# Sliding-window attention and gated MLP: values times probabilities once per pair of heads, in two PSUM banks shared with the transposes

## The chip, the cores and the metric

The kernel runs on one core of a Trainium2 chip, with its engines TensorE (PE; PEld is its loading of weights), VectorE (DVE), ScalarE (ACT), GpSimd (POOL) and the DMA queues that SyncE (SP) issues. The metric is the time of one execution on the device in microseconds; smaller is better.

## The reference

Attention with 4 batches, 8 heads, 768 positions and 64 elements a head. A query sees the 4 first keys (sinks) and the 128 keys that end with its own. The result, laid out as 512 columns a position, goes through an MLP with 1024 inner columns and a gate that comes from a convolution over three positions.

```python
scores = scale * np.matmul(q, k.transpose(0, 1, 3, 2))
is_sink = pos[None, :] < int(n_sink)          # n_sink = 4
rel = pos[:, None] - pos[None, :]
in_window = (rel >= 0) & (rel < int(window))  # window = 128
scores = np.where(is_sink | in_window, scores, -1000000000.0)
a = softmax(scores)
x = (a @ v) as (B, S, H * D)
h = np.maximum(x @ w_in, 0.0)
conv_out += conv_w[k] * hp[:, k:k + S, :]     # k = 0, 1, 2
out = (h * sigmoid(conv_out)) @ w_out
```

All is float32. Where the kernel wants float32 accuracy from one pass of PE, it splits an operand into a high and a low part (names ending in H and L) and adds three products; other float32 products take two passes.

## The kernel before, in words

`banded` works on pairs of heads, `g` = 0 to 15: 4 batches of 4 pairs (`NPAIR` = 4). A pair has 6 tiles of 128 queries, `t` = 0 to 5, in two halves of three tiles (`hf`, `u`). Batch 0 runs all first halves of its four pairs and then all second halves; later batches (`g >= NPAIR`) run a pair's two halves one behind the other. The main loop has one step `i` for each tile and three slots in a step: `scores` of tile i, `transp` of the tile before, `pv` of the tile before that (delays `D1` = 1, `D2` = 2).

- `scores(g, t)` makes scores of a tile for both heads (sc, L334 to L338), masks them on DVE (L502, L503), takes exponents on ACT (L506) and normalises on POOL (L511) into `pe`.
- `transp(g, t)` turns the two 128 x 128 blocks of probabilities with PE into a slot of `pts` in PSUM (L526), and one ACT copy (L528) brings them to the key tile's `pT` in SBUF. `pT` of key tile kt holds, for both heads, the block of query tile kt and that of query tile kt + 1, since the window reaches one tile back; POOL's two selects (L530, L532) cut the two triangles from the one block. At a half's last tile the sinks' probabilities are turned as well (`sT`, L540 or L548).
- `pv(g, t)` does nothing except at a half's last tile. There it multiplies values by the probabilities of the half's key tiles into `px`, one PSUM bank with 3 x 128 columns (L567): the values of one head are 64 columns of weights, so that the two heads lie in partitions 0 to 63 and 64 to 127. The sinks' products are added (L570). Key tile 2 is needed by both halves (query tiles 2 and 3), and has a `pT` for each.
- `xout` then copies px to the high part of x on ACT (xH, L345), and DVE subtracts for the low part (xL, L346).

In between, the loop places pieces of the MLP of the batch before (`fill`, from `Moe.pieces`): products with w_in (ph, L183), the gate on ACT, DVE and POOL (L190 to L201), products with w_out (po, L210). A batch's pieces are made when the `pv` of its last pair has been written down, and are spread over the next 24 steps; those of the last batch come at the end with no attention beside them. This written order is not yet the order of the engines: the program is built with a scheduler that lays out each engine's instructions by its own simulated times, and puts waits where tiles, buffers and PSUM banks require them.

PSUM has eight banks: two for sc, one for pts, one for px, two with tag h, two for po. `PTB` is the number of pT buffers.

Of the kernel before, what the change touches and what calls it, by code (L numbers as in the profile page):

```python
# [10 lines left out]
F32 = mybir.dt.float32  # L11
F32R = mybir.dt.float32r
# [5 lines left out]
P = 128  # L18
D = 64
NEG = 1.0e9  # L20
NS = 4
SP = 16
SR = 6 * NS
KW = P + NS
SW = 2 * P + NS
CH = 256
NT = CH // P
PTB = 6
RAWB = 4
PLAIN = 4  # L30
ORDER = [("k", 0), ("k", 1), ("q", 0), ("q", 1)]
# [6 lines left out]
def f(ap):  # L38
    return ap.bitcast(F32)
# [353 lines left out]
def banded(c):  # L393

    nc = c.nc
    m = Moe(c)
    A = Attn(c, m.x, KW, m.mp, m.ps)
    T = A.T
    NPAIR = c.H // 2
    NG = c.B * NPAIR  # L400
    cp = c.es.enter_context(c.tc.tile_pool(name="bc", bufs=1))
    ap, ps = A.ap, A.ps
# [30 lines left out]
    vsr = cp.tile([3 * SR, 3, NPAIR * P], F32R, name="vsr")  # L433
# [18 lines left out]
    A.settle = lambda: m.need(len(m.raws))  # L452
    st = [Ctx() for g in range(NG)]
    for s in st:
        s.pe, s.pT, s.raw, s.X = {}, {}, {}, [None, None]
    st[0].v = c.v_raw[0]

    jobs = [(g, half) for half in range(2) for g in range(NPAIR)]
# [18 lines left out]
            st[g].raw[nm, half] = load_half(c, g, nm, half, c.raw[asked[0] % RAWB])  # L477
            asked[0] += 1

    pts = ps.tile([P, 2, 2, P], F32, name="pts")  # L480

    def scores(g, t):
        s = st[g]
# [29 lines left out]
    def keytile(g, kt, hf):  # L513

        s = st[g]
        if (kt, hf) not in s.pT:
            s.pT[kt, hf] = ap.tile([P, 2, 2, P], F32, tag="pT", name=f"pT{g}_{kt}_{hf}", bufs=PTB)
        return s.pT[kt, hf]

    def transp(g, t):  # L520
        s = st[g]
        hf, u = divmod(t, 3)
        pt = pts[:, A.n % 2]
        A.n += 1
        for j in range(2):
            nc.tensor.transpose(pt[:, j, :], s.pe[hf][:, u, j, NS:KW], c.ident)  # L526
        own = keytile(g, t, hf)[:, :, 0]
        nc.scalar.copy(own, pt)  # L528
        if t:
            nc.gpsimd.affine_select(out=keytile(g, t - 1, hf)[:, :, 1], in_=own, pattern=[[0, 2], [-1, P]],  # L530
                                    compare_op=ALU.is_gt, fill=c.zero, base=0, channel_multiplier=1)
            nc.gpsimd.affine_select(out=own, in_=own, pattern=[[0, 2], [1, P]], compare_op=ALU.is_ge, fill=c.zero,  # L532
                                    base=0, channel_multiplier=-1)
        if u == 2:
            pk = m.ps.tile([P, P], F32 if g < NPAIR else F32R, tag="h", name=f"tk{g}_{t}", bufs=2)
            sinks = s.pe[hf].rearrange("p t h k -> p (t h) k")
            if g < NPAIR:
                sk = ap.tile([P, 6, SP], F32, tag="sk", name=f"sk{g}_{hf}")
                nc.scalar.copy(sk, sinks[:, :, 0:SP])
                nc.tensor.transpose(pk[0:6 * SP, :], sk.rearrange("p t k -> p (t k)"), c.ident)  # L540
                s.sT = ap.tile([6 * SP, P], F32, tag="sT", name=f"sT{g}_{hf}")
                nc.scalar.copy(s.sT, pk[0:6 * SP, :])  # L542
                return
            sk = ap.tile([P, 3, 6, NS], F32R, tag="sk", name=f"sk{g}_{hf}")
            sinks = sinks[:, :, 0:NS]
            nc.scalar.copy(sk[:, 0:3:2], sinks.rearrange("p (o t) k -> p o t k", o=1).to_broadcast([P, 2, 6, NS]))
            nc.vector.tensor_tensor(out=sk[:, 1], in0=sinks, in1=f(sk[:, 0]), op=ALU.subtract)
            nc.tensor.transpose(pk[0:3 * SR, :], sk.rearrange("p a t k -> p (a t k)"), c.identr)  # L548
            s.sT = ap.tile([3 * SR, P], F32R, tag="sT", name=f"sT{g}_{hf}")
            nc.scalar.copy(s.sT, f(pk[0:3 * SR, :]))  # L550

    def pv(g, t):

        s = st[g]
        hp = g % NPAIR
        hf, u = divmod(t, 3)
        if u < 2:
            return
        px = ps.tile([P, 3, P], F32, tag="px", name=f"px{g}_{hf}").rearrange("p t k -> p (t k)")
        first = 3 * hf  # L560
        tiles = range(first + 2, max(0, first - 1) - 1, -1)
        for kt in tiles:
            pT = s.pT.pop((kt, hf)).rearrange("p h a k -> p h (a k)")
            lo, hi = max(kt, first), min(kt + 1, first + 2)
            cols = slice(P * (lo - kt), P * (hi - kt) + P)
            for j in range(2):
                nc.tensor.matmul(px[D * j:D * j + D, P * (lo - first):P * (hi - first) + P], s.v[:, kt, j, :], pT[:, j, cols],  # L567
                                 start=(kt == tiles[0]), stop=False, skip_group_check=True)
        for w in range(1 - hf, 3):
            nc.tensor.matmul(px[:, P * w:P * w + P], (vsr if g >= NPAIR else c.vs)[:, w, P * hp:P * hp + P], s.sT, start=False, stop=(w == 2),  # L570
                             skip_group_check=True)
        A.xout(g, hf, px)

    kks = []

# [44 lines left out]
    cuts = {NSTB // 2: (0, 1, NSTB // 2), NSTB: (1, m.NCH, NSTB)}  # L620
# [3 lines left out]
    for i in range(NST + D2):  # L624
        if i < NST:
            n, g, t = steps[i]
# [15 lines left out]
        for slot in range(SLOTS):  # L642
            if slot == 0 and i < NST:
                scores(g, t)
            if slot == 1 and 0 <= i - D1 < NST:
                transp(*steps[i - D1][1:])
            if slot == 2 and 0 <= i - D2 < NST:
                pv(*steps[i - D2][1:])
                if i - D2 + 1 in cuts:
                    while fill:  # L650
                        fill.pop(0)()
                    lo, hi, span = cuts[i - D2 + 1]
                    fill = m.pieces(lo, hi)
                    rate = len(fill) / (span - 0.5)
                    acc = 0.0
            acc += rate / SLOTS
            while acc >= 1.0 and fill:
                fill.pop(0)()
                acc -= 1.0
            while todo and i + (slot + 1) / SLOTS >= todo[0][0]:  # L660
                todo.pop(0)[1]()
# [73 lines left out]
def attention_gated_mlp(ctx: ExitStack, tc: tile.TileContext, q, k, v, n_sink, window, w_in, conv_w, w_out, out):  # L735
# [33 lines left out]
    with tc.If(fast == 1) as cmp:  # L769
        with ExitStack() as es:  # L770
            c.es = es
            banded(c)
# [32 lines left out]
```

## Time and profile before

| what | value |
|---|---|
| median of 3 runs | 490.8 us (489.17 to 491.21) |
| profiled execution, its time | 491.53 us |
| profiled execution, its span | 489.8 us |
| mean granted TensorE clock | 0.991 |
| instructions | 10503 |
| busy share of PE, DVE, ACT, POOL | 93%, 70%, 70%, 64% |
| HBM read, written | 27.60 MB, 6.29 MB |

The span is from the first to the last instruction. A group's row gives the line, engine, operation, output and inputs, shapes and count, then busy us and the mean ns of one, then the idle time of the engine ahead of it and what ended it. Matmuls overlap, and their ends are modelled: what one costs is read from the distance of starts. In the timeline, neighbours of one kind are merged (x16), and a row in brackets tells the idle time before.

### The profile page before, as it was taken

Reading aid. Unit: us, or ns where it says so; the run is one execution under the profiler, and the core shown is the slowest. Engines: PE = TensorE matmul, PEld = TensorE weight load, DVE = VectorE, ACT = ScalarE, POOL = GpSimd, SP = SyncE. Lnnn points to the kernel's source line nnn. Section 1 sums busy time; section 2 is a strip of 40 time slices with the busy share of each in tenths; the row PEclk is TensorE's granted clock in tenths of the full one; section 3 lists DMA queues with packets and bytes.
Section 4 is the critical chain, followed back from the end, with each engine's and each line's share of the span. In section 5 each row is a group of like instructions: output and inputs, shape, how many; then the busy total and the mean of one; then the engine's idle time right before and its main releaser. Section 6 shows DMA issues by size and latency. Waiting matters only on the chain.

```text
span 489.8 us, 10503 instructions
## 1 busy us (share of the span) xinstructions
PE 457.6 (93%) x3149; PEld 388.8 (79%) x3149; DVE 343.8 (70%) x1211; ACT 344.3 (70%) x1087; POOL 314.0 (64%) x614
## 2 busy tenths in 40 slices
PE   1877698999999999999999999999999999999993
PEld 1644577778888888998888887898888888999982
DVE  4689989857768777776677778686776574655561
ACT  3888877869867978887768877785867664545541
POOL 3396688856876868695657667585765564444341
PEclk9999979999999999999999999999999999999999
DMA  5687744547234141433231421333120100101001
GB/s 145 188 250 205 187 146 84 135 91 184 52 81 115 62 115 33 101 96 83 73 86 35 107 68 34 71 92 85 45 58 8 45 2 1 44 1 43 26 20 51
DMA packets 87307, 41.01 MB, mean 84 GB/s; under 512 B 80161, under 2 KB 80185, under 8 KB 87241
## 3 DMA queue, kind: packets, MB, share of 16 engines
q1 hardware_dynamic: 87240, 40.25, 32.0%
q8 instruction: 27, 0.44, 0.4%
q14 instruction: 40, 0.32, 0.2%
HBM read 27.60 MB, written 6.29 MB: 69 GB/s over the span
## 4 chain that ended last, share of the span: by engine, by line
PE 83%; POOL 4%; DVE 3%; ACT 3%; DMA 3%; issue 2%; SPq 1%; DVEq 0%; ACTq 0%; POOLq 0%
PE ph L183 28%; PE po L210 27%; PE px L567 8%; PE pts L526 4%; PE sc L337 4%; PE sc L338 3%; PE px L570 2%; PE tq L271 2%; POOL pe L511 2%; PE sc L334 2%; PE tk L289 1%; DMA raw<-in_k_dram 1%; POOL wiL L122 1%; DMA sc_i<-in_window_dram 1%; POOL pT L530 1%
## 5 line engine op out<-in xcount | busy, mean ns | idle before, releaser
L210 PE MATMUL po<-woH,g 128*128 128x512 f32 x384 | 142.2, 410 | 1.2 <-POOL g L200 1.2
L183 PE MATMUL ph<-xH,wiH 128*128 128x258 f32 (+1 forms) x384 | 112.7, 293 | 1.2 <-ACT sT L542 1.2
L183 PE MATMUL ph<-xH,wiL 128*128 128x258 f32 (+1 forms) x384 | 110.0, 287 | 0.0
L183 PE MATMUL ph<-xL,wiH 128*128 128x258 f32 (+1 forms) x384 | 109.4, 285 | 0.0
L511 POOL TENSOR_SCALAR pe<-pe,sm 128x132 f32<-128x132 f32 (+1 forms) x192 | 86.0, 459 | 30.4 <-DVE sm L509 19.1
L200 POOL TENSOR_SCALAR g<-t 128x256 fp32r<-128x256 f32 x96 | 41.9, 437 | 79.1 <-DVE t L198 59.0
L506 ACT ACTIVATE pe<-pe,sm 128x132 f32<-128x132 f32 (+1 forms) x192 | 77.5, 407 | 16.6 <-DVE sm L503 15.2
L195 DVE SCALAR_TENSOR_TENSOR t<-hb,cw,t 128x256 f32<-128x256 f32 x96 | 55.5, 579 | 35.5 <-ACT t L194 34.4
L210 PEld LDWEIGHTS po<-woH,g 128*128 128x128 f32 x384 | 69.0, 189 | 12.1 <-POOL g L200 2.6
L183 PEld LDWEIGHTS ph<-xH,wiH 128*128 128x128 f32 x384 | 73.2, 191 | 6.6 <-ACT sT L542 2.0
L201 POOL TENSOR_TENSOR g<-t,g 128x256 fp32r<-128x256 f32 x96 | 74.3, 774 | 5.4
L210 PE MATMUL po<-woL,g 128*128 128x512 f32 x192 | 76.6, 399 | 0.0
L183 PEld LDWEIGHTS ph<-xH,wiL 128*128 128x128 f32 x384 | 73.3, 191 | 2.2
L183 PEld LDWEIGHTS ph<-xL,wiH 128*128 128x128 f32 x384 | 73.3, 191 | 0.9
L197 ACT ACTIVATE t<-t 128x256 f32<-128x256 f32 x96 | 40.3, 420 | 34.7 <-DVE t L196 34.4
L502 DVE COPY_PREDICATED sc<-before,sc 128x128 f32<-128x128 int32 x160 | 44.9, 291 | 25.7 <-PE sc L338 20.5
L198 DVE SCALAR_TENSOR_TENSOR t<-t,hb 128x256 f32<-128x256 f32 x96 | 47.0, 490 | 21.1 <-ACT t L197 20.2
L503 DVE CUSTOM_DVE_ANT_0 pe<-sc,m 128x132 f32<-128x132 f32 (+1 forms) x192 | 52.6, 288 | 10.1 <-PE sc L338 7.8
L196 DVE SCALAR_TENSOR_TENSOR t<-hb,cw,t 128x256 f32<-128x256 f32 x96 | 55.6, 579 | 4.4
L530 POOL TENSOR_SCALAR_AFFINE_SELECT pT<-pT 128x256 f32<-128x256 f32 x80 | 39.2, 490 | 29.5 <-ACT pT L528 25.2
L190 ACT ACTIVATE hb<-ph 128x258 f32<-128x258 f32 (+1 forms) x96 | 37.0, 385 | 29.3 <-PE ph L183 27.8
L194 ACT ACTIVATE t<-hb,cw 128x256 f32<-128x256 f32 x96 | 49.2, 513 | 7.1 <-POOL g L201 3.3
(123 smaller groups left out, 918.4 us busy)
## 6 DMA issues: line engine op xcount, KB each, us to landing
raw<-in_q_dram SPq DMA_DIRECT2D x64, 96.0 KB
raw<-in_k_dram SPq DMA_DIRECT2D x64, 96.0 KB
out_dram<-stm SPq DMA_DIRECT2D x24, 256.0 KB
kk<-kk SPq DMA_DIRECT2D x24, 198.0 KB
vraw<-in_v_dram SPq DMA_DIRECT2D x24, 192.0 KB
wi_0r<-in_moe_w_in_dram SPq DMA_DIRECT2D x2, 512.0 KB
wi_1r<-in_moe_w_in_dram SPq DMA_DIRECT2D x2, 512.0 KB
wi_2r<-in_moe_w_in_dram SPq DMA_DIRECT2D x2, 512.0 KB
```

The source lines that it names most:

```text
L183: nc.tensor.matmul(u.h[:, 0:W], w[:, cc, ff * P:(ff + 1) * P], x[:, cc, t0:t1], start=(i == 0), stop=(i == len(prods) - 1))
L194: nc.scalar.mul(a, prev, cw[:, 0, ff:ff + 1])
L195: nc.vector.scalar_tensor_tensor(out=e, in0=this, scalar=cw[:, 1, ff:ff + 1], in1=a, op0=ALU.mult, op1=ALU.add)
L196: nc.vector.scalar_tensor_tensor(out=a, in0=nxt, scalar=cw[:, 2, ff:ff + 1], in1=e, op0=ALU.mult, op1=ALU.add)
L198: nc.vector.scalar_tensor_tensor(out=a, in0=e, scalar=1.0, in1=this, op0=ALU.add, op1=ALU.mult)
L201: nc.gpsimd.tensor_tensor(out=u.g[:, 1], in0=a, in1=f(u.g[:, 0]), op=ALU.subtract)
L210: nc.tensor.matmul(po[:, 0:c.DM], u.g[:, a, tt * P:(tt + 1) * P], w[:, ff, :], start=(ff == 0 and i == 0), stop=(ff == NFF - 1 and i == 2))
L502: nc.vector.copy_predicated(pc[:, KW:SW], before.bitcast(I32), pc[:, 0:P])
L503: nc.vector.tensor_tensor_reduce(out=pe[:, j, cols], in0=pc[:, P:SW][:, cols], in1=mk, op0=ALU.add, op1=ALU.min, scale=1.0, scalar=3.0e38, ...
L506: nc.scalar.activation(pe[:, j, cols], pe[:, j, cols], AF.Exp, bias=sm[:, j:j + 1], scale=-1.0, accum_out=sm[:, 2 + 2 * j:3 + 2 * j])
L511: nc.gpsimd.tensor_scalar(pe[:, j, cols], pe[:, j, cols], sm[:, 8 + j:9 + j], 1.0, ALU.mult, ALU.mult)
L530: nc.gpsimd.affine_select(out=keytile(g, t - 1, hf)[:, :, 1], in_=own, pattern=[[0, 2], [-1, P]], compare_op=ALU.is_gt, fill=c.zero, base= ...
```

## The change

For later batches `pv` acts only at the pair's last tile (t = 5) and makes all six tiles of x at once, into `pb`, a PSUM tile of two banks (1024 columns): x takes columns 0 to 767. The last 256 columns, in the second bank, are `pts`, which held two slots before and holds one now. `px` is gone. Key tile 2 of a later pair has one pT in place of two, so a pair has six, all held until `pv`; `PTB` goes from 6 to 7. A product that would reach over the edge of the two banks is cut in two there (`cuts`). The sinks' probabilities of the first half are kept (`sT` for each half). The two halves of x are then copied out one behind the other. In batch 0 the halves stay as they were, with x in the first bank.

```diff
-PTB = 6
+PTB = 7
...
-    pts = ps.tile([P, 2, 2, P], F32, name="pts")
+    pb = ps.tile([P, 2 * T // 3, 2, P], F32, name="pb").rearrange("p t h k -> p (t h k)")
+    pts = pb[:, T * P:T * P + 2 * P].rearrange("p (h k) -> p h k", h=2)
...
     def keytile(g, kt, hf):
         s = st[g]
+        hf = hf if g < NPAIR else 0
...
     def transp(g, t):
-        pt = pts[:, A.n % 2]
-        A.n += 1
         for j in range(2):
-            nc.tensor.transpose(pt[:, j, :], s.pe[hf][:, u, j, NS:KW], c.ident)
+            nc.tensor.transpose(pts[:, j, :], s.pe[hf][:, u, j, NS:KW], c.ident)
         own = keytile(g, t, hf)[:, :, 0]
-        nc.scalar.copy(own, pt)
+        nc.scalar.copy(own, pts)
...
     def pv(g, t):
-        if u < 2:
+        if u < 2 or (g >= NPAIR and hf == 0):
             return
-        px = ps.tile([P, 3, P], F32, tag="px", name=f"px{g}_{hf}").rearrange("p t k -> p (t k)")
-        first = 3 * hf
-        tiles = range(first + 2, max(0, first - 1) - 1, -1)
-        for kt in tiles:
-            pT = s.pT.pop((kt, hf)).rearrange("p h a k -> p h (a k)")
-            lo, hi = max(kt, first), min(kt + 1, first + 2)
-            cols = slice(P * (lo - kt), P * (hi - kt) + P)
-            for j in range(2):
-                nc.tensor.matmul(px[D * j:D * j + D, P * (lo - first):P * (hi - first) + P], s.v[:, kt, j, :], pT[:, j, cols],
-                                 start=(kt == tiles[0]), stop=False, skip_group_check=True)
-        for w in range(1 - hf, 3):
-            nc.tensor.matmul(px[:, P * w:P * w + P], (vsr if g >= NPAIR else c.vs)[:, w, P * hp:P * hp + P], s.sT, start=False, stop=(w == 2),
-                             skip_group_check=True)
-        A.xout(g, hf, px)
+        first = 3 * hf if g < NPAIR else 0
+        begun = set()
+        for kt in range(t, max(0, first - 1) - 1, -1):
+            pT = s.pT.pop((kt, hf if g < NPAIR else 0)).rearrange("p h a k -> p h (a k)")
+            lo, hi = max(kt, first), min(kt + 1, t)
+            cuts = [(lo, hi)] if (lo - first) // 4 == (hi - first) // 4 else [(lo, lo), (hi, hi)]
+            for a, e in cuts:
+                bank = (a - first) // 4
+                for j in range(2):
+                    nc.tensor.matmul(pb[D * j:D * j + D, P * (a - first):P * (e - first) + P], s.v[:, kt, j, :],
+                                     pT[:, j, P * (a - kt):P * (e - kt) + P], start=bank not in begun, stop=False, skip_group_check=True)
+                begun.add(bank)
+        for w in range(max(first, 1), t + 1):
+            x = pb[:, P * (w - first):P * (w - first) + P]
+            nc.tensor.matmul(x, (vsr if g >= NPAIR else c.vs)[:, w % 3, P * hp:P * hp + P], s.sT[w // 3],
+                             start=False, stop=(w == t), skip_group_check=True)
+        for h in range(first // 3, hf + 1):
+            A.xout(g, h, pb[:, P * (3 * h - first):P * (3 * h - first) + 3 * P])
```

More of the change, by code (lines that the diff above doesn't have):

```diff
@@ L454, in banded @@
     for s in st:
-        s.pe, s.pT, s.raw, s.X = {}, {}, {}, [None, None]
+        s.pe, s.pT, s.sT, s.raw, s.X = {}, {}, {}, {}, [None, None]
     st[0].v = c.v_raw[0]
@@ L540, in transp @@
                 nc.tensor.transpose(pk[0:6 * SP, :], sk.rearrange("p t k -> p (t k)"), c.ident)
-                s.sT = ap.tile([6 * SP, P], F32, tag="sT", name=f"sT{g}_{hf}")
-                nc.scalar.copy(s.sT, pk[0:6 * SP, :])
+                s.sT[hf] = ap.tile([6 * SP, P], F32, tag="sT", name=f"sT{g}_{hf}")
+                nc.scalar.copy(s.sT[hf], pk[0:6 * SP, :])
                 return
@@ L548, in transp @@
             nc.tensor.transpose(pk[0:3 * SR, :], sk.rearrange("p a t k -> p (a t k)"), c.identr)
-            s.sT = ap.tile([3 * SR, P], F32R, tag="sT", name=f"sT{g}_{hf}")
-            nc.scalar.copy(s.sT, f(pk[0:3 * SR, :]))
+            s.sT[hf] = ap.tile([3 * SR, P], F32R, tag="sT", name=f"sT{g}_{hf}")
+            nc.scalar.copy(s.sT[hf], f(pk[0:3 * SR, :]))
     def pv(g, t):
```

## Prediction

> **What bounds the kernel now.** I read the page first: its share of busy time, its clock row and the chain that ended last.
>
> ```profile
> span 489.8 us, 10503 instructions
> PE 457.6 (93%) x3149; PEld 388.8 (79%) x3149; DVE 343.8 (70%) x1211; ACT 344.3 (70%) x1087; POOL 314.0 (64%) x614
> PEclk9999979999999999999999999999999999999999
> PE 83%; POOL 4%; DVE 3%; ACT 3%; DMA 3%; issue 2%; SPq 1%; DVEq 0%; ACTq 0%; POOLq 0%
> PE ph L183 28%; PE po L210 27%; PE px L567 8%; PE pts L526 4%; PE sc L337 4%; PE sc L338 3%; PE px L570 2%; PE tq L271 2%; POOL pe L511 2%; PE sc L334 2%; PE tk L289 1%; DMA raw<-in_k_dram 1%; POOL wiL L122 1%; DMA sc_i<-in_window_dram 1%; POOL pT L530 1%
> ```
>
> The chain runs on PE for 83% of the span, and 10% of the span is the work that the change touches: values times probabilities (px L567, 8%) and their sink part (L570, 2%). Then I asked for the busy time in stretches, because an average over 490 us hides stages.
>
> ```profile
> 20.00:60.00 40.00, 30.19 (x190) 20.54 (x188) 35.79 (x138) 34.46 (x114) 28.99 (x50) 1.00 0.81 224
> 60.00:120.00 60.00, 56.30 (x362) 45.49 (x363) 47.38 (x164) 46.42 (x145) 44.48 (x75) 0.94 0.53 129
> 120.00:200.00 80.00, 79.56 (x605) 69.28 (x604) 61.29 (x246) 65.52 (x226) 62.42 (x129) 1.00 0.35 82
> 200.00:410.00 210.00, 210.00 (x1513) 182.35 (x1512) 147.99 (x547) 153.15 (x498) 140.58 (x283) 1.00 0.24 60
> 410.00:480.00 70.00, 70.00 (x448) 62.80 (x447) 39.73 (x75) 33.72 (x79) 29.66 (x48) 1.00 0.06 24
> ```
>
> The columns after the length are busy PE, PEld, DVE, ACT, POOL, then clock, DMA share and GB/s. Until 120 us (batch 0) PE has gaps; from 120 us on it has none. The change touches later batches alone in its arithmetic, and those lie in the stretch without gaps. So there only two things count: microseconds of PE work taken away, and new waits for which PE has nothing else at hand.
>
> **The change part by part.** *The matmuls themselves: nothing.* Groups by form, with out and in, count, busy and mean ns:
>
> ```profile
> L567 PE MATMUL px<-pT,vraw 128*64 128x256 f32 x256 | 35.1, 380 | 0.0
> L567 PE MATMUL px<-pT,vraw 128*64 128x128 f32 x192 | 23.8, 292 | 1.9 <-POOL pT L532 1.9
> L570 PE MATMUL px<-sT,vsr 72*128 72x128 f32 x60 | 11.1, 278 | 0.0
> ```
>
> 448 passes over 16 pairs are 28 a pair: 7 products a head, two heads, two passes each for fp32. Before, a pair has key tiles 2,1,0 (128, 256 and 256 columns) in its first half and 5,4,3,2 (128, 256, 256, 128) in its second: three of 128 and four of 256. After, 5,4,3,2,1,0 would be one of 128 and five of 256, but key tile 3 reaches from x tile 3 into x tile 4, which is where the first bank ends, so it is cut in two 128s: again three of 128 and four of 256. The sinks' products are 2+3 before and 5 after. Copies of transposes, selects, both x copies and all DMAs keep their number and size. Nothing is moved past SP's queue; on POOL's the selects stay at their steps. The price of the arithmetic is 0, and no cover is needed for that.
>
> *The bursts: a gain.* What shrinks is how often PE turns from the other shapes (128*128) to this one (128*64) and back: 24 bursts in the 12 later pairs become 12. PE's timeline around two bursts:
>
> ```profile
> 412.49 0.28 PE L183 MATMUL ph<-xH,wiL 128*128 128x258 f32 x1
> 412.61 0.28 PE L183 MATMUL ph<-xL,wiH 128*128 128x258 f32 x1
> 412.82 1.52 PE L567 MATMUL px<-pT,vraw 128*64 128x128 f32 x16
> 414.27 0.55 PE L570 MATMUL px<-sT,vsr 72*128 72x128 f32 x3
> ...
> 185.71 1.30 PE L567 MATMUL px<-pT,vraw 128*64 128x128 f32 x12
> 186.94 0.33 PE L337 MATMUL sc<-kk,X 128*128 128x128 f32 x1
> ```
>
> Read starts, since ends are modelled. A second half takes 414.27 - 412.82 = 1.45 us for 8 passes of 256 and 8 of 128 columns; a first half 186.94 - 185.71 = 1.23 us for 8 of 256 and 4 of 128. The difference, 0.22 us, is four passes of 128, so 0.055 us each, and 0.11 us for one of 256. That makes 8 x 0.11 + 8 x 0.055 = 1.32 us of the 1.45, and leaves 0.13 us on the way out. On the way in, 412.82 comes 0.21 us after 412.61 where ph products follow each other at 0.12: another 0.09 us. A burst has a fixed 0.22 us, and 12 fewer are worth 2.6 us of PE. Some bursts are broken in two already (221.09 and 223.01 below), and a longer one may be broken more often; I take off one or two extra breaks and keep 2.3 us. Ends: 0 if the long bursts are broken as often as there were halves, 3.5 us if today's breaks go too.
>
> *One slot for transposes: nothing.* The two slots of pts share one bank, and the trace has a place that shows what that is worth:
>
> ```profile
> 41.40 0.37 ACT L528 COPY pT<-pts 128x256 f32<-128x256 f32 x1
> 41.91 0.41 PE L526 MATMUL pts<-ident,pe 128*128 128x128 f32 x2 [0.92 <-ACT pT L528]
> ```
>
> The transposes of 41.91 go to the other slot, and still they sat 0.92 us until the copy of the slot before them was out (41.40 + 0.37 = 41.77). Two slots already behave as one. Over the whole run this wait is 0.9 us of PE, in this one place. One slot costs 0; the ends are a gain of 0 and a loss of 0.9.
>
> *The shared bank: a new wait, taken at 0.* The same row says what comes: whatever shares a bank is put in order. Four things now do, at the end of each later pair. The transposes and the copy of the next pair's tile 0 come ahead of the values' products, and these, with the four reads of x, ahead of the transposes of the next pair's tile 1. The reads:
>
> ```profile
> L345 ACT CAST xH<-px 128x384 fp32r<-128x384 f32 x32 | 15.3, 478 | 8.8 <-PE px L570 8.7
> L346 DVE TENSOR_TENSOR xL<-px,xH 128x384 fp32r<-128x384 f32 x32 | 17.7, 552 | 9.0 <-ACT xH L345 8.9
> ```
>
> The second half of x lies over both banks, so its reads come behind the first's: 2 x (0.48 + 0.55) = 2.1 us in a row. Behind the waiting transposes stand the copy to pT, the selects on POOL and the next pair's values; ACT's second copy waits for DVE's first subtraction, with exponents behind it. Uncovered, this is 12 x 2.1 = 25 us. What covers it is MoE work of the batch before. The trace has a harder case of it, at the first pair of batch 2, whose sinks came late:
>
> ```profile
> 204.52 0.66 PE L567 MATMUL px<-pT,vraw 128*64 128x128 f32 x6
> 211.38 0.23 PE L570 MATMUL px<-sT,vsr 72*128 72x128 f32 x1
> 216.72 0.23 PE L570 MATMUL px<-sT,vsr 72*128 72x128 f32 x1
> 221.09 1.51 PE L567 MATMUL px<-pT,vraw 128*64 128x128 f32 x14
> 223.01 0.43 PE L567 MATMUL px<-pT,vraw 128*64 128x128 f32 x2
> ...
> 203.00:217.00 14.00, 14.00 (x106) 12.52 (x106) 10.96 (x44) 11.72 (x43) 13.23 (x24) 1.00 0.21 58
> ```
>
> The first half's x hung from 204.5 to 216.7, the second half's products waited for its bank, and PE was busy 14.00 of 14.00 us. A wait of 12 us in attention cost PE nothing; one of 2 to 3 us should not either. Ends: 0, and 0.5 us a pair (6 us) where the order laid out beforehand and the chip disagree.
>
> The Trainium skill ("PSUM — Partial Sum Buffer", section "PSUM bank collisions raise a hardware error") says that two engines must not be in one bank and quadrant at once, disjoint columns and reads included, so that software has to order them. The 0.92 us above agrees; by that rule alone, with no cover, the sum would be the 25 us loss.
>
> *The end: 0.7 us.* The first half of x of a batch's last pair now comes out with the second. Only in batch 3 does MoE work stand directly behind it:
>
> ```profile
> 407.04 0.38 PE L526 MATMUL pts<-ident,pe 128*128 128x128 f32 x2
> 409.20 0.41 POOL L532 TENSOR_SCALAR_AFFINE_SELECT pT<-pT 128x256 f32<-128x256 f32 x1
> 410.26 0.40 PE L210 MATMUL po<-woH,g 128*128 128x512 f32 x1
> 414.86 0.48 ACT L345 CAST xH<-px 128x384 fp32r<-128x384 f32 x1 [1.71 <-PE px L570]
> 415.37 0.56 DVE L346 TENSOR_TENSOR xL<-px,xH 128x384 fp32r<-128x384 f32 x1 [1.32 <-ACT xH L345]
> ```
>
> Before, the last products start at 412.82 although their last key tile is ready at 409.6: PE was filled with ph and po, some of it of batch 3 already. After, that filler must come from batch 2's rest and from the three quarters of a unit that need no last pair (9 of 12 ph products, 1.1 us, in each of two buffers). From the last product to x's low part there are 1.7 us (414.27 to 415.93), which those 2.2 us cover. I take 0.7 us for what does not fit; ends 0 and 3.3 us (the 5.8 us from 407.04 to 412.82, less the 2.5 us that the 28 passes then take).
>
> *Also:* values are multiplied one half later, so a new batch's sinks (216.72) are no longer awaited by a first half; PE had cover there, 0. The seventh pT slot replaces what six live key tiles need; 0.
>
> **The sum** against the profiled execution's 491.5 us (span 489.8): -2.3 + 0 + 0 + 0.7 = -1.6, so 489.9. That execution is 0.7 us over the median of the runs shown, 490.8 (489.17 to 491.21); on the median's scale I predict 489.2 us.
>
> **The rivals.** (1) *Nothing reaches the clock:* the order of all engines is laid out again with every change, so bursts are broken elsewhere and the 2.3 us go under: 490 to 492. For it: breaks such as 221.09 and 223.01; 2.3 us is 0.5%, about what a measurement of this kernel can tell from no change. (2) *Slower, by the shared bank:* PE stands at the next pair's transposes while x is read. It eats up the gain at 1.6 / 12 = 0.13 us a pair, can be told from no change at (1.6 + 2.5) / 12 = 0.34, and at 1 us a pair the sum is +10.4 us, or 501. Against it: the 14.00 of 14.00. For it: POOL was 13.23 of 14 there, so a late tile is not caught up at once. (3) *More than the bursts:* today's breaks go as well, and all 3.5 us and more come without the loss at the end: 485 to 487. Against it: PE's stops for a late select inside px, which fewer bursts could save, are the 1.9 us in the row above, and the waits up to 120 us hold all of them:
>
> ```profile
> PE px L567 <- POOL pT L532: 1.9, 3, 0.8
> ```
>
>  (4) *Batch 0 is laid out otherwise.* Its clock digit of 7 is a stretch at a lower clock, 0.94 in the mean of 60 to 120 us; with it gone or doubled, the time moves by up to 0.06 x 60 = 3.6 us either way. It widens each case.
>
> **How the numbers follow.** My forecast, 1 to 3.5 us saved, has 0.50 (487 to 490); no visible change 0.24; the shared bank 0.18 (493 to 502); more than the bursts 0.08. The range leaves out about 0.1 at each side: the lower end, 485, is in case 3; the upper, 496, is the bank at 0.6 us a pair. The likeliest case's own range is 486.5 to 491. Faster by over 0.5% means under 488.3: 0.4 of the forecast's 0.50, all of case 3 and a little of case 1, 0.32. Slower by over 0.5%, above 493.3: most of case 2 and some of case 4, 0.20. Within: 0.48.
>
> **What would show it.** Groups: L567 still 448 passes, 256 of 256 and 192 of 128 columns. Timeline: about 20 bursts in place of 32, those of later pairs with 28 passes over some 2.5 us. Waits of PE after 120 us: nothing for pts or px beyond 1 us; a row "pts waits for DVE xL" of several us is rival 2. Stretches: 120 to 410 still without gaps, but about 2 us shorter. At the end: no PE gap over 1 us between the last px and the next ph. I am wrong if PE shows gaps after 120 us, if the bursts stay about 30, or if the first 120 us move by more than 2 us.

## The result: slower, 501.8 us for 490.8, and the profile after

| | before | after |
|---|---|---|
| median (lowest to highest, 4 runs after) | 490.77 us (489.17 to 491.21) | 501.84 us (500.45 to 502.52) |
| ratio, 95% interval | | 1.0225 [1.0204, 1.0246] |
| profiled execution, its span | 491.53, 489.8 us | 500.45, 498.7 us |
| mean granted clock | 0.991 | 0.993 |

The prediction was 489.2 us (485 to 496). The time lies outside the range and on the other side; its rival 2 had the size ("at 1 us a pair ... 501"). That match is partly luck: 1 us a pair was an example there, and the cause it named, the shared bank, could not be told from nothing in the runs below. Lines are shifted in the changed kernel: the values' products are L570 and the sinks' L575, the transposes L527, their copy to pT L529, the selects L531 and L533; px and pts are both called pb.

The page: span, busy engines, the chain that ended last.

```profile
span 498.7 us, 10463 instructions
PE 456.4 (92%) x3149; PEld 387.2 (78%) x3149; DVE 342.9 (69%) x1211; ACT 339.7 (68%) x1087; POOL 314.2 (63%) x614
PE 72%; DVE 9%; ACT 6%; POOL 5%; DMA 4%; issue 3%; SPq 1%; ACTq 0%; DVEq 0%; POOLq 0%
```

The same 3149 matmuls, and less busy time on each of PE, DVE and ACT than before; but the chain runs on PE for 72% of the span in place of 83%, and on DVE and ACT for 15% in place of 6%. So the work has not grown: PE waits more, at the end of chains that run over these two. The stretches say where (length, then busy PE, PEld, DVE, ACT, POOL, clock, DMA share, GB/s):

```profile
120.00:200.00 80.00, 76.20 (x562) 66.09 (x561) 58.88 (x228) 61.03 (x212) 57.50 (x117) 1.00 0.32 77
200.00:410.00 210.00, 206.63 (x1500) 180.08 (x1499) 146.99 (x552) 149.43 (x495) 137.43 (x278) 1.00 0.24 62
410.00:490.00 80.00, 79.21 (x507) 69.61 (x506) 42.89 (x82) 38.33 (x92) 36.46 (x63) 1.00 0.06 21
```

Before, PE had 79.56, 210.00 and all of 70.00 us in these stages. Now 3.8, 3.4 and 0.8 us are idle, at full clock. The groups by form that answer to those of the prediction (busy us and mean ns of one, then the idle time ahead and who ended it):

```profile
L570 PE MATMUL pb<-pT,vraw 128*64 128x256 f32 x256 | 36.9, 388 | 0.0
L570 PE MATMUL pb<-pT,vraw 128*64 128x128 f32 x192 | 18.8, 287 | 3.4 <-POOL pT L533 3.4
L527 PE MATMUL pb<-ident,pe 128*128 128x128 f32 x192 | 38.0, 278 | 5.6 <-ACT pT L529 3.9 <-DVE xL L346 1.6
L345 ACT CAST xH<-pb 128x384 fp32r<-128x384 f32 x32 | 15.2, 476 | 21.9 <-PE pb L575 17.5 <-DVE xL L346 4.4
L346 DVE TENSOR_TENSOR xL<-pb,xH 128x384 fp32r<-128x384 f32 x32 | 17.7, 554 | 17.9 <-ACT xH L345 17.6
```

The products are what was forecast, 256 and 192 passes. New are the idle times: the transposes wait for the copy pT and for xL, 5.5 us over the whole run (4.3 of them before 120 us, where PE has gaps in both kernels), and the reads of x wait for each other and for the sinks' products, 21.9 us of ACT (8.8 before) and 17.9 us of DVE (9.0 before).

PE's waits from 120 us on (engine and line, awaited, us in total, times, longest), of before and then, up to 480 us, five of the ten rows of after. The 1.2 us of before stand at its very end; after has them too, at 491 us, beyond its rows:

```profile
PE po L210 <- POOL g L200: 1.2, 1, 1.2
PE sc L337 <- PE tq L271: 0.4, 1, 0.4
```

```profile
PE po L210 <- POOL g L200: 2.0, 3, 1.2
PE sc L337 <- DVE sm L505: 1.9, 4, 1.1
PE pb L527 <- ACT pT L529: 0.8, 2, 0.4
PE ph L183 <- ACT hb L190: 0.6, 2, 0.4
...
PE pb L527 <- DVE xL L346: 0.4, 1, 0.4
```

There is no one large wait. It is many small ones, for DVE, ACT and POOL in turn, and few of them name x. One later pair, the last of batch 1, shows how they can hang together (timeline: start, us, engine, line; of the rows of all engines those that matter here):

```profile
207.88 0.78 PE L575 MATMUL pb<-sT,vsr 72*128 72x128 f32 x5
208.69 0.48 ACT L345 CAST xH<-pb 128x384 fp32r<-128x384 f32 x1 [0.33 <-PE pb L575]
209.42 0.55 DVE L346 TENSOR_TENSOR xL<-pb,xH 128x384 fp32r<-128x384 f32 x1
210.00 0.48 ACT L345 CAST xH<-pb 128x384 fp32r<-128x384 f32 x1 [0.83 <-DVE xL L346]
210.52 0.56 DVE L346 TENSOR_TENSOR xL<-pb,xH 128x384 fp32r<-128x384 f32 x1
211.13 0.44 PE L527 MATMUL pb<-ident,pe 128*128 128x128 f32 x2 [0.43 <-DVE xL L346]
212.10 0.37 ACT L529 COPY pT<-pb 128x256 f32<-128x256 f32 x1
212.52 0.44 PE L527 MATMUL pb<-ident,pe 128*128 128x128 f32 x2 [0.40 <-ACT pT L529]
216.25 0.28 DVE L505 CUSTOM_DVE_ANT_0 pe<-sc,m 128x128 f32<-128x128 f32 x1
...
216.59 0.39 PE L337 MATMUL sc<-kk,X 128*128 128x260 f32 x1 [1.06 <-DVE sm L505]
```

The four reads of x come one behind the other, 208.69 to 211.08. The next transposes start at 211.13, 0.05 us after the last read, and PE stood 0.43 us for them; the transposes behind these stood 0.40 us for the copy of the first. At 216.59 scores wait for DVE for 1.06 us. The last of these I connect with the first only by time; the first is the wait that the prediction took at 0, and the second stands right behind it.

This pair is the extreme one. In the other ten later pairs that have transposes behind them, these start 1.7 to 3.9 us after the last read of x (for the first, 143.57 after 140.16), and PE does other work up to them. So the order that the tile forces is in every pair, but PE stands still for it, by its own row above, for only 0.4 us from 120 us on; the other stalls come further along the queues.

**A sum over the trace.** Ends of matmuls are modelled, so short stalls hide in "busy". For the comparison below I used starts: from 120 us on, the distance from one PE start to the next less the usual one (231 ns for po, 119 for ph and sc, 110 for the sinks, 60 for transposes, 107.5 and 54 for a pass of 256 and 128 columns). What is over 150 ns is a *stall*; what stands at a change between px and another shape is a *turn* (its number is that of the bursts, twice).

| kernel | stalls us (number) | turns us (number) | 60 to 150 ns, us |
|---|---|---|---|
| before | 2.1 (3) | 8.7 (62) | 11.2 |
| after | 14.0 (28) | 5.5 (36) | 12.9 |

Stalls +11.9, turns -3.2, the rest +1.7 make +10.4 us. The profiled executions differ by 8.9 us and the medians by 11.1. Up to 120 us PE loses 50.0 us in both.

### The profile page after: what moved, and what is told of

Its sections match the earlier page's. It is cut to its first block, busy times and chain, and to the rows that moved or that the text cites. A ratio compares the mean times of both kernels' runs of the same rounds, so it can differ in the third digit from the quotient of the medians.

```text
span 498.7 us, 10463 instructions
## 1 busy us (share of the span) xinstructions
PE 456.4 (92%) x3149; PEld 387.2 (78%) x3149; DVE 342.9 (69%) x1211; ACT 339.7 (68%) x1087; POOL 314.2 (63%) x614
## 4 chain that ended last, share of the span: by engine, by line
PE 72%; DVE 9%; ACT 6%; POOL 5%; DMA 4%; issue 3%; SPq 1%; ACTq 0%; DVEq 0%; POOLq 0%
PE po L210 25%; PE ph L183 24%; PE pb L570 7%; PE pb L527 3%; PE sc L337 3%; PE sc L338 3%; PE pb L575 2%; PE sc L334 2%; PE tq L271 2%; DVE stm L114 1%; POOL pe L513 1%; PE tk L289 1%; DVE t L195 1%; POOL wiL L122 1%; DMA wi_2r<-in_moe_w_in_dram 1%
## 5 line engine op out<-in xcount | busy, mean ns | idle before, releaser
L210 PE MATMUL po<-woH,g 128*128 128x512 f32 x384 | 139.7, 409 | 4.6 <-POOL g L200 4.2
L183 PE MATMUL ph<-xH,wiL 128*128 128x258 f32 (+1 forms) x384 | 108.6, 283 | 0.0
L513 POOL TENSOR_SCALAR pe<-pe,sm 128x132 f32<-128x132 f32 (+1 forms) x192 | 84.6, 451 | 34.5 <-DVE sm L511 24.0
L200 POOL TENSOR_SCALAR g<-t 128x256 fp32r<-128x256 f32 x96 | 43.2, 451 | 94.1 <-DVE t L198 68.5
L195 DVE SCALAR_TENSOR_TENSOR t<-hb,cw,t 128x256 f32<-128x256 f32 x96 | 55.8, 582 | 38.0 <-ACT t L194 37.5
L196 DVE SCALAR_TENSOR_TENSOR t<-hb,cw,t 128x256 f32<-128x256 f32 x96 | 52.8, 550 | 4.1
L531 POOL TENSOR_SCALAR_AFFINE_SELECT pT<-pT 128x256 f32<-128x256 f32 x80 | 40.2, 503 | 16.5 <-ACT pT L529 16.2
```

The costliest lines, as they stand in the source:

```text
L183: nc.tensor.matmul(u.h[:, 0:W], w[:, cc, ff * P:(ff + 1) * P], x[:, cc, t0:t1], start=(i == 0), stop=(i == len(prods) - 1))
L195: nc.vector.scalar_tensor_tensor(out=e, in0=this, scalar=cw[:, 1, ff:ff + 1], in1=a, op0=ALU.mult, op1=ALU.add)
L196: nc.vector.scalar_tensor_tensor(out=a, in0=nxt, scalar=cw[:, 2, ff:ff + 1], in1=e, op0=ALU.mult, op1=ALU.add)
L200: nc.gpsimd.tensor_scalar(u.g[:, 0], a, 1.0, 1.0, ALU.mult, ALU.mult)
L210: nc.tensor.matmul(po[:, 0:c.DM], u.g[:, a, tt * P:(tt + 1) * P], w[:, ff, :], start=(ff == 0 and i == 0), stop=(ff == NFF - 1 and i == 2))
L513: nc.gpsimd.tensor_scalar(pe[:, j, cols], pe[:, j, cols], sm[:, 8 + j:9 + j], 1.0, ALU.mult, ALU.mult)
```

## The experiments

Four theories go by letters in the expectations. **A**: the bank that x and the transposes share. **B**: the first halves come late, with the second ones. **C**: the scheduler's new layout of all queues, by chance. **D**, formed after the first four kernels: not the bank but the *tile*. x and the transposes are parts of one PSUM tile, and the uses of one tile come in written order, wherever in it they lie. Medians in us, ratios to the kernel before on the same chip with 95% intervals; stalls and turns as in the table above.

### Which part costs?

*e1_share_only*: the shared tile and bank, but two halves as before; a later pair's second half lies at columns 384 to 767, over both banks (so with the cut of key tile 3).

```diff
-        if u < 2 or (g >= NPAIR and hf == 0):
+        if u < 2:
             return
-        first = 3 * hf if g < NPAIR else 0
+        first = 3 * hf
+        base = 3 * hf if g >= NPAIR else 0
...
-        for h in range(first // 3, hf + 1):
-            A.xout(g, h, pb[:, P * (3 * h - first):P * (3 * h - first) + 3 * P])
+        A.xout(g, hf, pb[:, P * base:P * base + 3 * P])
```

> The halves are multiplied when the kernel before does it (24 bursts in later batches, a pT of its own for key tile 2 in each half, 6 pT), but in the new layout: the second half of a later pair lies over the edge of the two banks and shares the second with the one slot for transposes. Theory A (the 11 us come from the shared bank: the next pair's transposes stand until x is read): most of the loss stays, since 12 pairs still share; the burst is shorter by 1.2 us and the first half's reads (1.0 us) are out of the way, so about half of it: 494 to 500 us. Theory B (the 11 us come from multiplying both halves late: six pT held, x late): 489 to 492. Theory C (any new layout of the queues moves the time by a per cent): anywhere from 486 to 497, with PE gaps at other places than in the changed kernel.

Measured: 500.79, 1.0208 [1.0187, 1.0230]; stalls 12.8 (26), turns 6.5 (48). Nearly all of the loss is there without late halves.

*e2_defer_only*: the kernel before, with px and pts as they were, but both halves multiplied at the pair's end.

```diff
-        if u < 2:
+        if u < 2 or (g >= NPAIR and hf == 0):
             return
...
+        for h in (0, 1) if g >= NPAIR else (hf,):
+            px = ps.tile([P, 3, P], F32, tag="px", name=f"px{g}_{h}").rearrange("p t k -> p (t k)")
```

> Both halves of a later pair are multiplied at its last tile, with six pT and PTB = 7 as in the changed kernel, but one half after the other in the old px bank, and transposes have their own bank with two slots. Theory A: no loss, 488.5 to 492.5 us, transposes of the next pair's tile 1 may start before x is read. Theory B: the loss stays, 498 to 503. Theory C: 486 to 497.

Measured: 493.82, 1.0068 [1.0045, 1.0092]; stalls 2.0 (2), turns 10.7 (74). It did not do what it was made for. PE's timeline:

```profile
144.33 1.30 PE L571 MATMUL px<-pT,vraw 128*64 128x128 f32 x12
148.55 0.34 PE L574 MATMUL px<-sT,vsr 72*128 72x128 f32 x2
154.14 1.52 PE L571 MATMUL px<-pT,vraw 128*64 128x128 f32 x16
```

The first half (12 passes) still runs 10 us ahead of the second: the scheduler pulled it forward, since nothing holds it. Of the 3.2 us that it lost, 2.0 are turns, 74 for 62.

*e4_one_slot*: two halves, one tile of two banks, but all of x in the first bank and one slot of transposes in the second. No bank is shared. Against e1:

```diff
-        base = 3 * hf if g >= NPAIR else 0
+        base = 0
```

> As the kernel before in its order of work, with one slot for transposes alone in the second bank and both halves of x in the first bank, so that nothing is shared. Theories A and B: 489 to 492 us; the step of the prediction that costs one slot at 0 is right if it is within 1 us of the kernel before. If one slot were the cause, 496 or more. Theory C: 486 to 497.

Measured: 495.72, 1.0104 [1.0080, 1.0129]; stalls 8.3 (15), turns 6.5 (48). 5 us are lost with no bank shared. Neither A nor B explains that.

*e6_transposes_aside*: after, but the transposes of a pair's tiles 0 and 1 go to the two buffers with tag h, so that they need not wait for x.

```diff
+        pt = m.ps.tile([P, 2, P], F32, tag="h", name=f"tp{g}_{t}", bufs=2) if g > NPAIR and t < 2 else pts
         for j in range(2):
-            nc.tensor.transpose(pts[:, j, :], s.pe[hf][:, u, j, NS:KW], c.ident)
+            nc.tensor.transpose(pt[:, j, :], s.pe[hf][:, u, j, NS:KW], c.ident)
```

> The changed kernel, except that in batches 1 to 3 (from the second pair of batch 1 on) the transposes of tiles 0 and 1 go to a PSUM tile of tag h (two banks, used by the MLP's first product and the preparation) and no longer share a bank with x. Theory A: the loss goes, less what two more users of tag h cost (0 to 3 us); with the 2.3 us of the bursts 487 to 493 us. Theory B: 498 to 503. Theory C: 486 to 503.

Measured: 506.59, 1.0335 [1.0312, 1.0358]; stalls 12.7 (28), turns 9.5 (58). Worse, and outside all three ranges. The buffers it takes are those of ph and of the preparation of q and k, which now stand behind the transposes (ph, tk and tq wait for their copy for 1.3 us from 120 us on); it replaces one wait by another and decides nothing.

### Bank or tile?

*e7_one_tile*: the kernel before with its two slots and no cut; x in the first bank and the slots in the second, as they were apart before, but in one tile. This is the whole edit:

```diff
-    pts = ps.tile([P, 2, 2, P], F32, name="pts")
+    pb = ps.tile([P, 8, P], F32, name="pb").rearrange("p t k -> p (t k)")
+    pts = pb[:, 4 * P:8 * P].rearrange("p (s h k) -> p s h k", s=2, h=2)
...
-        px = ps.tile([P, 3, P], F32, tag="px", name=f"px{g}_{hf}").rearrange("p t k -> p (t k)")
+        px = pb[:, 0:3 * P]
```

> The kernel before, except that px and pts are cut from one PSUM tile of two banks: x in the first bank, the two slots for transposes in the second; nothing shares a bank, bursts and pT as before. Theory D (accesses of different engines to one PSUM tile are put in written order whatever their banks, and that makes the stalls): as with one slot and x in one tile (495.7 us), 494 to 497, PE stalls over 150 ns after 120 us of 6 to 10 us, and no transposes between a values' burst and the end of its x reads. Theory A (the shared bank alone): 489 to 492. Theory C (layout by chance): 486 to 497, with transposes in between as before.

*e8_own_tile*: the kernel before with one slot for transposes, in a tile of its own.

```diff
-    pts = ps.tile([P, 2, 2, P], F32, name="pts")
+    pts = ps.tile([P, 2, P], F32, name="pts")
...
-        pt = pts[:, A.n % 2]
-        A.n += 1
+        pt = pts
```

> The kernel before, except that pts is one slot and not two, in a tile and bank of its own. Theory D and the prediction's step on the slot: no loss, 489 to 492 us. If the single slot is the cause: 494 to 497. Theory C: 486 to 497.

Measured: e7 495.70, 1.0084 [1.0055, 1.0113], stalls 8.3 (15), turns 6.5 (48), as in e4. e8 490.74, 0.9994 [0.9969, 1.0019], stalls 1.5 (2), turns 8.8 (62), as before. So the second slot is worth nothing, and the 5 us (4.1 by the ratio of e7) come with the one tile alone. The same stalls stand in e4 and e7, one by one, some 1.4 us apart, so the two are one layout and not two witnesses. PE's rows of e7 name no wait for xL from 120 us on; the first is again for the copy of transposes:

```profile
PE pb L527 <- ACT pT L529: 2.0, 4, 0.9
```

Timeline of e7, the rows of pb alone:

```profile
136.81 0.38 PE L527 MATMUL pb<-ident,pe 128*128 128x128 f32 x2
137.22 0.37 ACT L529 COPY pT<-pb 128x256 f32<-128x256 f32 x1 [0.21 <-PE pb L527]
140.49 1.52 PE L568 MATMUL pb<-pT,vraw 128*64 128x128 f32 x16
141.94 0.55 PE L571 MATMUL pb<-sT,vsr 72*128 72x128 f32 x3
142.59 0.46 ACT L345 CAST xH<-pb 128x384 fp32r<-128x384 f32 x1
143.08 0.56 DVE L346 TENSOR_TENSOR xL<-pb,xH 128x384 fp32r<-128x384 f32 x1 [0.33 <-ACT xH L345]
146.87 0.38 PE L527 MATMUL pb<-ident,pe 128*128 128x128 f32 x2
```

From the first product at 140.49 to the end of the last read at 143.64 there are no transposes, though these write another bank. That holds for all later pairs of e7 and of after.

*e5_two_tiles* and *e5b_mid*: after, with x tiles 0 to 3 in a tile `pa` of one bank, and x tiles 4 and 5 with the transposes in a second tile `pq`. e5 does all products and then both reads; e5b finishes the second tile first.

```diff
+    pa = ps.tile([P, 4 * P], F32, name="pa")
+    pq = ps.tile([P, 4 * P], F32, name="pq")
+    pts = pq[:, 2 * P:4 * P].rearrange("p (h k) -> p h k", h=2)
...
+            groups = [(pq, 4, [4, 5]), (pa, 0, [0, 1, 2, 3])]
...
+        for do in (products, sinks, out):
+            for x in groups:
+                do(*x)
```

> The changed kernel with its two banks as two PSUM tiles: x tiles 0 to 3 in the one, x tiles 4 and 5 and the slot for transposes in the other; products into the second come first, the sinks at the end, and x is copied out by bank (256 and 512 columns), the second bank first. 12 bursts in later batches. The transposes of the next pair's tile 1 wait for two reads of 256 columns in place of four of 384. Theory D: most of the stalls go and the bursts' 2 to 3 us show: 488 to 494 us. Theory A: the bank is still shared, so a part of the loss stays, 492 to 498. Theory C: 486 to 503.

> As the kernel with two tiles, but the second bank is finished with its sinks and read while PE still multiplies into the first bank, so that the transposes hardly wait; PE turns its shape twice more a pair (12 x 0.2 = 2.4 us). Theory D and theory A: within 2 us of the kernel with two tiles, better if the reads still hold the transposes, worse by 2.4 if they do not. Theory C: 486 to 503.

Measured: e5 498.04, 1.0118 [1.0062, 1.0174], stalls 6.5 (15), turns 9.9 (68); e5b 496.99, 1.0110 [1.0051, 1.0168], 5.9 (14), 9.9 (68). D's range for e5 (488 to 494) was missed. The stalls are halved, as D has it, but the bursts break up (68 turns for 36), which gives back 4.4 us. More than one tile is left in the loss.

### Late halves, bursts and the cut

*e9_defer_forced*: e2 with an order edge: a later pair's products may be issued only after its last transposes.

```diff
-            nc.tensor.transpose(pt[:, j, :], s.pe[hf][:, u, j, NS:KW], c.ident)
+            s.turned = nc.tensor.transpose(pt[:, j, :], s.pe[hf][:, u, j, NS:KW], c.ident)
...
+                    with c.tc.issue_after(s.turned.ins):
+                        nc.tensor.matmul(px[D * j:D * j + D, P * (lo - first):P * (hi - first) + P], s.v[:, kt, j, :], pT[:, j, cols],
```

> Both halves of a later pair late and nothing else: px, and two slots for transposes, each in a tile and bank of its own as in the kernel before; one pT for key tile 2, PTB = 7; the products of both halves are queued on PE behind the transposes of tile 5 (order of issue only), so that the scheduler cannot pull the first half forward as it did in the run that only asked for it. Theory B (late halves cost by themselves): 495 to 503 us. Theory D (one tile for x and transposes costs) with late halves free: 489 to 494. Theory C (layout by chance): 486 to 497.

Measured: 495.95, 1.0085 [1.0062, 1.0108]; stalls 5.0 (11), turns 10.5 (68). Now B gets its test, and late halves cost 4.5 us by themselves, with px and pts as before: 2.9 us more stalls and 1.8 us more turns.

*e10_two_tiles_kept*: e5 with order edges that hold the products of a burst behind its first one.

```diff
+                    with (c.tc.issue_after(head[0].ins) if head else ExitStack()):
```

> The kernel with two tiles (x tiles 0 to 3; x tiles 4, 5 and the slot), now with all products of a pair queued behind its first one, so that the 28 passes stay together as in the changed kernel. If the breaks of the bursts were what the kernel with two tiles paid (px in and out 9.9 us of PE, against 5.5 in the changed kernel): 2 to 4 us less than its 498.0, 493 to 496. If the late halves and the shared second bank are: 497 to 500. Theory C: 486 to 503.

Measured: 497.25, 1.0123 [1.0099, 1.0147]; stalls 10.0 (18), turns 6.7 (46). The bursts hold (46 turns), and the stalls are back.

*e11_before_kept*: the same edges in the kernel before.

```diff
+                with (c.tc.issue_after(head.ins) if head is not None else ExitStack()):
```

> The kernel before with only an order of issue added: a half's products are queued behind its first. At 0.22 us a burst, some 7 breaks fewer after 120 us give 1 to 1.5 us: 488.5 to 490.5 us if the fixed price of a burst is what it seems; 491 to 493 if the later start of the burst costs more. Theory C: 486 to 497.

Measured: 490.76, 0.9982 [0.9967, 0.9998]; turns 8.7 (62). The edges kept nothing together here, so this says only that they cost nothing.

*e12_one_tile_cut*: e4 (one tile, no bank shared) with the cut of key tile 3 that e1 and after have.

```diff
-            cuts = [(lo, hi)] if (lo - first + base) // 4 == (hi - first + base) // 4 else [(lo, lo), (hi, hi)]
+            cuts = [(lo, hi)] if not (g >= NPAIR and kt == 3) else [(lo, lo), (hi, hi)]
```

> The run with one slot and x in one tile but separate banks (495.7 us), with one product more a pair: key tile 3 of a later pair's second half is cut in two 128s as it is where x lies over the edge of the banks (48 passes more, the same columns). If the further 5 us of the run that shares the bank (500.8) come from the sharing: 495 to 497. If they come from the cut or from the layout: 499 to 502.

Measured: 500.08, 1.0168 [1.0147, 1.0189]; stalls 12.8 (26), turns 6.4 (48): to a tenth those of e1, where the bank is shared as well. What the shared bank adds to the shared tile is 0.7 us by the medians and 0.0040 (2.0 us) by the ratios, whose intervals touch: not told from nothing. But the cut, 48 more passes at equal columns, brings 4.4 us over e4 by the medians, 0.0064 (3.1 us) by the ratios.

*e13_before_cut*: that cut in the kernel before, with two tiles.

```diff
+            for a, e in ([(lo, lo), (hi, hi)] if g >= NPAIR and kt == 3 else [(lo, hi)]):
+                cols = slice(P * (a - kt), P * (e - kt) + P)
```

> The kernel before with key tile 3 of a later pair's second half cut in two 128s: 48 passes more, the same columns, everything else as before. If the cut costs by its passes: 494 to 496 us. If it costs only where the chain is already tight or by the layout of the queues: 489.5 to 492.

*e14_other_cut*: e4 with key tile 1 cut in place of 3, as many more passes.

```diff
-            cuts = [(lo, hi)] if (lo - first + base) // 4 == (hi - first + base) // 4 else [(lo, lo), (hi, hi)]
+            cuts = [(lo, hi)] if not (g >= NPAIR and kt == 1) else [(lo, lo), (hi, hi)]
```

> One tile, separate banks, one slot (495.7 us without a cut, 500.1 with key tile 3 cut), with key tile 1 of the first half cut in its place: 48 passes more as well. If a cut in one tile costs by itself: 499 to 501. If the 4.4 us were the layout that this one cut happened to give: 494 to 498.

Measured: e13 494.93, 1.0074 [1.0047, 1.0100], stalls 2.9 (4), turns 10.6 (76). e14 495.05, 1.0080 [1.0052, 1.0107], stalls 6.9 (13), turns 6.5 (48), the time of e4 and e7 without a cut. So 48 passes have no price of their own: one cut costs 4 us in two kernels and the other none. In e13 the 4 us go with 14 more turns and in e12 with 11 more stalls, that is, with another layout of the queues. That speaks for C, by about 4 us; that cutting key tile 3 has a price wherever it is done, and key tile 1 has none, is not excluded.

*e15_order_only*: the kernel before, two tiles, with order edges that give PE the order which one tile forces: products after the newest transposes, the next transposes after the sinks' products. Without one tile, transposes do not wait for the reads of x.

```diff
+        with (c.tc.issue_after(A.sink) if A.sink else ExitStack()):
+            for j in range(2):
+                A.turned = nc.tensor.transpose(pt[:, j, :], s.pe[hf][:, u, j, NS:KW], c.ident).ins
...
+        with c.tc.issue_after(A.turned):
+            tiles = range(first + 2, max(0, first - 1) - 1, -1)
...
+                A.sink = nc.tensor.matmul(px[:, P * w:P * w + P], (vsr if g >= NPAIR else c.vs)[:, w, P * hp:P * hp + P], s.sT, start=False, stop=(w == 2),
```

> The kernel before (own tiles, two slots), with PE's order between transposes and values kept as written: a half's products are queued behind the transposes written ahead of them, and later transposes behind its sinks; nothing waits for the reads of x. If the order alone makes the loss of one tile: 494 to 497 us. If the transposes' wait for the reads makes it: 489 to 492. In between: both.

Measured: 489.35, 0.9970 [0.9948, 0.9992]; stalls 2.5 (3), turns 8.4 (56). Timeline of e15, rows of px and pts:

```profile
131.83 1.52 PE L570 MATMUL px<-pT,vraw 128*64 128x128 f32 x16
133.28 0.55 PE L573 MATMUL px<-sT,vsr 72*128 72x128 f32 x3
133.88 0.46 ACT L345 CAST xH<-px 128x384 fp32r<-128x384 f32 x1
134.77 0.38 PE L528 MATMUL pts<-ident,pe 128*128 128x128 f32 x2
135.15 0.56 DVE L346 TENSOR_TENSOR xL<-px,xH 128x384 fp32r<-128x384 f32 x1
```

and all of PE's waits from 120 us on:

```profile
PE po L210 <- POOL g L200: 2.0, 3, 1.2
```

The transposes start at 134.77, ahead of xL's read at 135.15: what e7 forbids. With the same order between products and transposes on PE, the 5 us are not there. So in e4 and e7 it is not this order alone which costs, but what one tile adds to it. That is two waits: the transposes' for the reads of x, and the products' for the copy of the newest transposes (in e15 some products start before that copy has ended, in e7 none). No run parts the two.

*e16_order_chain*: e15 with each product of a burst behind the one before it, to hold bursts together as well.

```diff
+                    with (c.tc.issue_after(head) if head else ExitStack()):
+                        head = nc.tensor.matmul(px[D * j:D * j + D, P * (lo - first):P * (hi - first) + P], s.v[:, kt, j, :], pT[:, j, cols],
```

> The run that keeps PE's order between transposes and values (489.35 us), with each product of a half also queued behind the one before it. If keeping the order is a gain in itself: 488 to 490 us, ratio under 0.998. If that run's 1.6 us were the spread that any new layout brings: anywhere from 489 to 496.

Measured: 490.99 (486.96 to 492.26), 1.0002 [0.9984, 1.0019]. No gain; e15's 0.3% is within what a new layout does. No kernel here clearly beats the one before.

## Why the prediction was wrong, point by point

**The matmuls, 0: right as arithmetic, incomplete as a price.** 256 and 192 passes, as counted. But the cut which keeps this count was costed by its columns alone; with the layout that follows, it cost 4.0 (e13) and 4.4 us (e12), where a like cut of key tile 1 cost none (e14).

**The bursts, -2.3 us: right.** Turns fell from 62 to 36 and from 8.7 to 5.5 us: -3.2, or 0.12 us a turn, where the prediction had 0.22 us a burst in and out. The Trainium skill ("TensorEngine Tiling (Array Packing)", section "Tiling Modes") says that a change of the tiling mode drains TensorE; these products alone have tiles of 128*64, and the 0.12 us agree with a drain, for which the page has no price. PE did save what was forecast. It was paid out again.

**One slot, 0: right.** e8 is 0.9994. Its transposes wait for the copy of the slot before them for 0.8 us over the whole run (0.9 before):

```profile
L525 PE MATMUL pts<-ident,pe 128*128 128x128 f32 x192 | 40.0, 281 | 3.2 <-POOL pe L511 2.3 <-ACT pT L527 0.8
```

**"The shared bank: a new wait, taken at 0": the step that failed,** in its cover and in its cause. *The cover*: the prediction argued from 203 to 217 us before, where x hung for 12 us and PE stayed at 14.00 of 14.00, that "one of 2 to 3 us should not either" cost anything. What hung there was a chain that the transposes did not stand behind. PE's timeline of before in that stretch:

```profile
204.52 1.30 PE L567 MATMUL px<-pT,vraw 128*64 128x128 f32 x12
...
207.36 0.38 PE L526 MATMUL pts<-ident,pe 128*128 128x128 f32 x2
...
210.47 0.38 PE L526 MATMUL pts<-ident,pe 128*128 128x128 f32 x2
...
213.69 0.38 PE L526 MATMUL pts<-ident,pe 128*128 128x128 f32 x2
...
216.72 0.23 PE L570 MATMUL px<-sT,vsr 72*128 72x128 f32 x1
```

With x hanging, three tiles' transposes went on. In the changed kernel the transposes are what stands, and behind them the copies, the selects, the next values. The prediction had written down this queue and the uncovered 25 us, and then put an example without the queue in its place. Its reads of x were 2.4 us (208.69 to 211.08) for 2.1 forecast; the stalls from 120 us on grew by 11.9 us, 1.0 us a pair, though not by this wait alone. The sign that it gave for rival 2, a row "pts waits for DVE xL" of several us, did not come: the row has 0.4 us. *The cause*: the row at 41.91 us was read as a bank that orders its users. The two slots were in one bank and in one tile, so the row could not tell which. The Trainium skill's rule on banks ("PSUM — Partial Sum Buffer", "PSUM bank collisions raise a hardware error") holds for the bank, but e4 and e7 lose 5 us with two banks, and truly sharing one adds nothing that e1 and e12 could tell.

**The end, +0.7 us: right in size, by another wait.** From 410 us on PE is idle for 0.79 us, 0 before. Its waits there are two of ph at the start of batch 3, 0.6 us together, and the first is this. They are not for x's low part, as forecast, but for ACT's copy of ph to hb:

```profile
424.45 0.40 PE L183 MATMUL ph<-xL,wiH 128*128 128x258 f32 x2
425.27 0.39 PE L183 MATMUL ph<-xH,wiH 128*128 128x258 f32 x1 [0.42 <-ACT hb L190]
```

**"Values are multiplied one half later ...; PE had cover there, 0": wrong.** Forced alone (e9), late halves cost 4.5 us. Why is open: x's halves then follow each other through one px, and 28 passes come at one time; no run parts the two.

**The sum.** By the single steps: one tile +5.0 (e7, e4), late halves +4.5 (e9), a cut 0 to +4.4 (e14, e12), turns -3.2 (the trace); 6.3 to 10.7 of 11.1 us. The turns are partly counted twice there, since the times of e7 and e9 hold turns of their own (-2.2 and +1.8 us). In stalls alone it is +6.2 for one tile, +2.9 for late halves and -1.4 to +4.5 for a cut, 7.7 to 13.6 for the measured 11.9. They need not add: e10, which takes after apart into two tiles with its bursts held, still loses 5.8 us to the kernel before, and e1 loses 10.2 without late halves. That the one tile costs 4 to 5 us in the kernel before is shown, since it is e7's whole edit; through which of its waits, and how much of it by the layout that follows from them, is not (e13 moves by 0.0074 with its tiles apart). How much of the other 6 is late halves and how much the layout around the cut is not settled; either alone can be more than half of it.

## What to carry to other kernels

A buffer cut from a larger PSUM tile takes over the order of all its users, in other banks too; give every user that must run free its own tile, even where the space would fit in one. Before an example from the trace is taken as cover for a new wait, look who stands in the queue behind it: here a stuck end of a chain cost a full engine nothing, and a tile shared with the head of the next pair cost 4 to 5 us. And a saving of 0.5% on the engine that bounds is no larger than what a new layout of the queues can do by itself, so it is forecast as "no change" until a run says otherwise.

## What the runs showed that was not expected

- At equal columns and equal instructions on all other engines, cutting one product in two moved the time by +4.0 us (e13) and another by none (e14): what seems to be the layout alone is worth 0.7 to 0.8%.
- Stalls hide in PE's busy time: the stretches show 8.0 us without PE from 120 us on (3.8 + 3.4 + 0.8), the distances of starts 14.0 us.
- What is written late need not run late: e2's first halves went 10 us ahead of their second ones, until an order edge held them (e9).
- Lines that the change does not touch stand longer too. POOL's wait for the gate's part on DVE (in total, times, longest, over the run) was at most 2.9 us before,

```profile
POOL g L200 <- DVE t L198: 59.0, 40, 2.9
```

and up to 8.4 us after. The 8.4 us end at 428.27, at the first gate of batch 3, whose ph products come behind the late x of the last pair; for the other long ones (5.2 us at 404.5) no run parts the cause:

```profile
POOL g L200 <- DVE t L198: 68.5, 42, 8.4
```
